# Float64 weights to fp32 by bytes on ScalarE, first slices ahead of the rows, even folds queued later, in a spectral two-MLP kernel

## The chip, the cores and the metric

One core of one Trainium2 chip. The metric is the device time of one launch in microseconds (us), the median of several runs; beside it stands one profiled execution, whose trace is read here.

## What is computed

```python
X = np.fft.fft(np.fft.fft(x, axis=1), axis=2).real      # x: 2 x 3008 x 256, fp32
x = X.reshape(6016, 256)
h = x @ w_in;  x = (np.maximum(h, 0) ** 2) @ w_out      # layer 1: 256 -> 2048 -> 256
h = x @ w_in2; y = (h - np.tanh(h)) @ w_out2            # layer 2: the same sizes
```

The weights arrive as float64. They have to become fp32 on the chip before anything else can use them.

## The kernel before

**Stages.** The 3008-point transform is done with matmuls against cosine and sine tables, on rows of `x` that have been added and subtracted ("folded") so that few distinct rows remain. The 256-point transform along the other axis is multiplied into layer 1's weights. Layer 1 runs over 8 blocks of about 376 columns (4 for each batch) and over 16 slices of 128 hidden units; layer 2 runs over the same blocks and slices, with its weights prepared during the last part of layer 1. Nearly every fp32 product is made of three matmuls on rounded halves, a high part and the remainder.

**The start.** `load_x` brings the rows of one third (two DMAs of 512 KB, added together on VectorE and GpSimd), `load_table` a table (752 KB), `fold` folds. The first five steps of a fold give the odd rows `xo`; the later steps (L319 to L328) give the even rows `xf`. `dft_pair` multiplies the odd rows with the tables, `pair_evac` takes the result out of PSUM into `uv`.

**One slice of weights.** `load_raw` loads a slice (512 KB, two 32-bit words for each number) into one of four `stage` buffers. `conv_abs` (ScalarE, L219) makes `val`, the high word's magnitude scaled so that its exponent fits; `val` has three buffers. `conv` (VectorE) shifts the low word right by 29 (L227), joins these bits with the shifted `val` (L229) and puts the sign in (L231). After L231 the stage buffer is free, and the next DMA for it may start. Then TensorE transforms the slice (`transform_in`, L247), ScalarE takes the high parts (L235, L250) and VectorE the remainders (L238, L255); `middle_load` moves one column by DMA, and `middle_add` and `clear_middle` on GpSimd finish it.

**One step of layer 1.** `front` multiplies slice and columns (TensorE, L352 to `w`); `mid` combines them on VectorE (L490 `pb`, L491 and L492 `h`), then ScalarE makes relu, the squared high part `gh` and the square (L498, L499, L500); `late` makes the remainder `gl` (L509; VectorE for block 0's first eight slices, GpSimd for all later ones); `back` multiplies by the second weights (L520). The first three slices skip the combination (`vneg`, L496). The slices 2 to 15 are converted and split while the steps of block 0 and 1 already run (`MADE` says at which step). The table `STEPS` sets the order: block 0's slices 0 to 3, block 1's 16 slices, block 0's slices 4 to 15, then block 2 to 7.

**Background work.** `bg0` finishes the even rows (L319 to L328, then `split_even`), `bg1` loads and folds the second batch (accumulating DMAs on GpSimd's queue, L288), `bg3` (`make_w2`) converts layer 2's 16 slices. A scheduler orders the instructions of each engine by readiness; `tc.issue_after(ins)` puts the instructions of its block that run on the engine of `ins` behind `ins` in that engine's order. Here `ins` is the latest L492, on VectorE, so ScalarE, GpSimd and SP are not held by it.

Of the kernel before, what the change touches and what calls it, by code (L numbers as in the profile page):

```python
# [138 lines left out]
def spectral_mlps(  # L139
# [62 lines left out]
    def wt_alloc(layer, f):  # L202
        wt[f] = main.tile([128, 4, 256], F32R, tag=f"wt{f}", name=f"wt{layer}_{f}")
# [2 lines left out]
        wt_alloc(2, f)  # L206
        sp.dma_start(f32(wt[f]).rearrange("p a n -> p (a n)"), saved[f])

    def load_raw(layer, f, eng=sp):
        t = stage()  # L210
        eng.dma_start(t.bitcast(I32), (w1 if layer == 1 else w2)[f].bitcast(I32))
        raw[layer, f] = t.bitcast(I32).rearrange("p (n t) -> p n t", t=2)

    def conv_abs(layer, f):
        v = main.tile([128, 512], F32, tag="val", name="val", bufs=3)
        val[layer, f] = v
        return act.activation(v, raw[layer, f][:, :, 1].bitcast(F32), AF.Abs, scale=2.0**-112)  # L219

    def conv(layer, f):

        r = raw.pop((layer, f))
        lo, hi = r[:, :, 0], r[:, :, 1]
        y = main.tile([128, 512], I32, tag="p", name="cy")
        u = val[layer, f].bitcast(I32)
        dve.tensor_scalar(y, lo, 29, None, ALU.logical_shift_right)  # L227
        yield
        dve.scalar_tensor_tensor(u, u, 3, y, ALU.logical_shift_left, ALU.bitwise_or)  # L229
        yield  # L230
        dve.scalar_tensor_tensor(u, hi, -(2**31), u, ALU.bitwise_and, ALU.bitwise_or)  # L231
        yield

    def split_hi(f, i, src):
# [5 lines left out]
    def transform_in(f, p):  # L240


        v = val[1, f]
        for m in range(2):
            for kt in range(2):
                cs = slice(kt * 128, (kt + 1) * 128)
                pe.matmul(p[:, m, 384:], wtab[:, kt, m, :], v[:, cs], start=(kt == 0), stop=(kt == 1))  # L247
# [94 lines left out]
    def load_table(blk, t):  # L342
        c = BLOCKS[blk][1]
        u = ring(f"tab{t}")
        sp.dma_start(f32(u)[:, :, :NC[c]], tabs_d[c][t])
        tab.setdefault(blk, []).append(u)
# [216 lines left out]
    def make_w2():  # L563

        for f in range(2):
            load_raw(2, f)
        yield
        for f in range(NF):
            conv_abs(2, f)
            yield  # L570
            yield from conv(2, f)
            if f + 2 < NF:
                load_raw(2, f + 2)
            v = val[2, f].rearrange("p (i n) -> p i n", i=2)
            u = main.tile([128, 2, 2, 256], F32R, tag="stage", name="w2", bufs=4)
            act.copy(u[:, :, 0], v)
            yield
            dve.tensor_tensor(u[:, :, 1], v, f32(u[:, :, 0]), ALU.subtract)
            sp.dma_start(saved[f], f32(u).rearrange("p i h n -> p (i h n)"))
            yield  # L580
            if f % 2 == 0:
# [12 lines left out]
            yield  # L594
            dve.tensor_tensor(u[:, 1], y, f32(u[:, 0]), ALU.subtract)
            sp.dma_start(sums_d[f // 2], f32(u).rearrange("p h n -> p (h n)"))
            yield
# [148 lines left out]
    yt = {}  # L746


    def weights1(f, p):

        wt_alloc(1, f)
        transform_in(f, p)
        split_hi(f, 2, val[1, f][:, 256:])
        split_transformed_hi(f, p)
        split_lo(f, 2, val[1, f][:, 256:])
        split_transformed_lo(f, p)

    pool.memset(sign, -1.0)
    pool.memset(sign[0:1], 1.0)
# [4 lines left out]
    for f in range(2):  # L764
        wps[0, f] = psw()

    for t in range(3):
        load_x(0, t)
        if t == 2:
            load_raw(1, 0)  # L770
            conv_abs(1, 0)
        load_table(0, t)
    sp.dma_start(wtab, wtab_d[:, :, :, :])
    for f in range(1, 5):
        load_raw(1, f)
    folds = [fold(0, t) for t in range(3)]
    step(folds[0], 5)
    step(folds[1], 5)
    step(conv(1, 0))
    step(folds[2], 5)  # L780
    for t in range(3):
        dft_pair(0, t)
    load_raw(1, 5)
    conv_abs(1, 1)
    weights1(0, wps[0, 0])
    middle_load(0)
    step(conv(1, 1))
    conv_abs(1, 2)
    pe0 = pair_evac(0)
    step(pe0, 1)  # L790
    n = NC[BLOCKS[0][1]]
    vneg = ring("vneg")
    for i in range(2):
        act.activation(vneg[:, i, :n], f32(uv[0][0][:, 1, i, :n]), AF.Copy, scale=sign)
    weights1(1, wps[0, 1])
    middle_load(1)
    step(conv(1, 2))
    conv_abs(1, 3)
    step(pe0)
    middle_add(0)  # L800

# [26 lines left out]
    for i in range(-2, NS - 2):  # L828
        blk, f = STEPS[i] if i >= 0 else (0, i)
        if i == max(MADE) + 2:  # L830
            wstack.close()
            pools["w"] = wstack.enter_context(tc.tile_pool(name="psb", bufs=2, space=PSUM))
        look(i + 2)
        if i in MADE:
            p = wps[STEPS[i + 2]]
            w = MADE[i]
            wt_alloc(1, w)
            transform_in(w, p)
            split_transformed_hi(w, p)

        if (blk, f) in DFT:
            for b2 in DFT[blk, f]:
                if b2 == 4:
                    step(bg1)
                    for t in range(3):
                        dft_pair(4, t)
                    step(pair_evac(4))
                else:
                    step(bg0 if b2 < 4 else bg2)
                    dft_mm(b2)  # L850
                    dft_evac(b2)
            look(i + 3)
        mids = mid(*STEPS[i + 2])
        step(mids, 1)
        if i >= 0:
            back(blk, f)
        if i >= 0 and ends(blk, f):
            evac(blk, blk == 0 and f == NF - 1)
        step(mids)
        if i >= -1:  # L860
            late(*STEPS[i + 1])

        if i + 4 in MADE and i + 4 > 1:
            load_raw(1, MADE[i + 4])
        if i in MADE:
            split_transformed_lo(w, p)
            split_hi(w, 2, val[1, w][:, 256:])
        if i + 2 in MADE and i + 2 > -1:
            conv_abs(1, MADE[i + 2])
        if i in MADE:  # L870
            split_lo(w, 2, val[1, w][:, 256:])
            middle_load(w)
        if i == -2:
            middle_add(1)
        if i - 1 in MADE:
            middle_add(MADE[i - 1])
        if i + 1 in MADE and i + 1 > -2:
            step(conv(1, MADE[i + 1]))

        if i >= 8:  # L880
            with tc.issue_after(last_mid[0].ins):
                if i < NF + HALF:
                    step(bg0, 1)
                elif i < 3 * NF:
                    step(bg1, 2)
                else:
                    if blk == 3:
                        step(bg2, 1)
                    step(bg3, 2)
        if blk == NBLK - 1:  # L890
            if f > 0:
                restore(f - 1)
            if f >= 8:
# [65 lines left out]
```

## Time and profile before

| | |
|---|---|
| median of 3 runs | 1008.41 us (1007.89 to 1009.72) |
| profiled execution, its own time | 1006.97 us |
| its span in the trace | 1005.1 us |
| TensorE busy | 963.3 us, 96% |
| VectorE busy | 787.4 us, 78% |
| ScalarE busy | 726.7 us, 72% |
| GpSimd busy | 251.6 us, 25% |
| chain that ended last | 80% TensorE, 12% VectorE, 3% issue, 2% ScalarE, 2% DMA |

TensorE is busy nearly all the time, so the time is its work plus what it waits, plus what it loses at a lower granted clock. A share over the whole span hides where that is: the stages have different limits, and are read one by one. The profile names TensorE PE (its weight loads PEld), VectorE DVE, ScalarE ACT, GpSimd POOL, and SP the queue that issues most DMAs.

### The profile page before, as it was taken

How to read it: one execution, taken by the hardware profiler on the slowest of the kernel's cores; microseconds unless marked ns; L12 is line 12 of the kernel's file. 1: busy time of each engine (PE TensorE's matmuls, PEld its weight loads, DVE VectorE, ACT ScalarE, POOL GpSimd, SP SyncE). 2: the span in 40 equal slices, each digit the busy share in tenths (PEclk: the TensorE clock that was granted, in tenths of full speed). 3: DMA queues.
4: the chain of work that ended last, by engine and by line, in shares of the span. 5: the costliest groups of instructions: out<-in, count | busy, mean ns of one | idle time of the engine just before them, and what ended most of it. 6: DMA issues, size and time to landing. Idle time of an engine off the chain costs nothing.

```text
span 1005.1 us, 15446 instructions
## 1 busy us (share of the span) xinstructions
PE 963.3 (96%) x5542; PEld 950.5 (95%) x5542; DVE 787.4 (78%) x1483; ACT 726.7 (72%) x1289; POOL 251.6 (25%) x171
## 2 busy tenths in 40 slices
PE   4998899899999999999999999999999999999998
PEld 3888898899999999999999999999999999999998
DVE  6999679757988688997576978769787797877766
ACT  2886767787888778897866767667676676766665
POOL 1144614653566546565500000000000000000000
PEclk9999999999999999999999999999999999999999
DMA  8674240205332422417620100001000010000000
GB/s 308 212 228 126 53 142 25 32 1 217 130 130 106 145 85 109 175 73 274 207 94 1 62 1 30 34 1 62 1 32 31 1 63 1 3 29 1 32 1 31
DMA packets 36332, 82.66 MB, mean 82 GB/s; under 512 B 7328, under 2 KB 21152, under 8 KB 36256
## 3 DMA queue, kind: packets, MB, share of 16 engines
q1 hardware_dynamic: 35280, 79.34, 22.5%
q0 software_dynamic: 976, 2.34, 1.4%
q8 instruction: 43, 0.70, 0.3%
q14 instruction: 33, 0.27, 0.1%
HBM read 55.97 MB, written 25.69 MB: 81 GB/s over the span
## 4 chain that ended last, share of the span: by engine, by line
PE 80%; DVE 12%; issue 3%; ACT 2%; DMA 2%; POOL 0%; SPq 0%; DVEq 0%; POOLq 0%; ACTq 0%
PE w L352 32%; PE a L352 29%; PE a L520 18%; DVE pb L490 2%; DVE h L491 2%; DVE h L492 1%; DMA p<-x 1%; DVE val L231 1%; DVE val L229 1%; DMA stage<-w 1%; ACT gh L499 1%; DVE p L321 1%; DVE wt L238 1%; PE w L247 1%; DMA mcol<-wt 0%
## 5 line engine op out<-in xcount | busy, mean ns | idle before, releaser
L509 POOL TENSOR_TENSOR gl<-h,gh 128x752 fp32r<-128x752 f32 (+1 forms) x120 | 230.0, 1925 | 195.2 <-ACT h L500 135.3
L352 PE MATMUL a<-gh,wt 128*128 128x376 f32 (+1 forms) x1024 | 259.7, 335 | 0.0
L520 PE MATMUL a<-gh,wt 128*128 128x376 f32 (+1 forms) x1024 | 204.4, 341 | 15.1 <-ACT gh L499 5.8
L520 PEld LDWEIGHTS a<-gh,wt 128*128 128x128 f32 x1024 | 179.4, 191 | 21.0 <-ACT gh L499 8.7
L352 PEld LDWEIGHTS a<-gh,wt 128*128 128x128 f32 x1024 | 184.7, 188 | 0.0
L352 PE MATMUL a<-gl,wt 128*128 128x376 f32 (+1 forms) x512 | 171.7, 335 | 0.0
L352 PE MATMUL w<-x,sums 128*128 128x376 f32 (+1 forms) x768 | 163.5, 334 | 0.0
L352 PE MATMUL w<-uv,wt 128*128 128x376 f32 (+1 forms) x777 | 157.1, 337 | 1.7 <-POOL wt L259 1.0
L498 ACT ACTIVATE h<-h 128x752 f32<-128x752 f32 (+1 forms) x125 | 103.8, 831 | 59.8 <-DVE h L492 59.1
L673 DVE TENSOR_TENSOR gl<-h,gh 128x376 fp32r<-128x376 f32 (+1 forms) x256 | 138.2, 545 | 11.2 <-ACT gh L671 10.6
L671 ACT CAST gh<-h 128x376 fp32r<-128x376 f32 (+1 forms) x256 | 129.3, 507 | 18.5 <-DVE h L669 17.6
L667 ACT ACTIVATE tanh<-h 128x376 f32<-128x376 f32 (+1 forms) x192 | 99.3, 519 | 56.6 <-DVE h L663 51.9
L352 PEld LDWEIGHTS w<-uv,wt 128*128 128x128 f32 x777 | 136.8, 190 | 2.8 <-POOL wt L259 1.3
L669 DVE TENSOR_TENSOR h<-h,tanh 128x376 f32<-128x376 f32 (+1 forms) x192 | 106.4, 555 | 40.0 <-ACT tanh L667 34.7
L352 PEld LDWEIGHTS w<-x,sums 128*128 128x128 f32 x768 | 135.5, 188 | 0.2 <-ACT u L701 0.2
L490 DVE SCALAR_TENSOR_TENSOR pb<-ub,w,w 128x376 f32<-128x376 f32 (+1 forms) x125 | 75.1, 601 | 56.5 <-PE w L352 48.6
L520 PE MATMUL a<-gl,wt 128*128 128x376 f32 (+1 forms) x512 | 109.1, 336 | 0.5 <-POOL gl L509 0.5
L500 ACT ACTIVATE h<-h 128x752 f32<-128x752 f32 (+1 forms) x128 | 106.8, 834 | 3.0
L499 ACT ACTIVATE gh<-h 128x752 fp32r<-128x752 f32 (+1 forms) x128 | 106.9, 835 | 2.9
L663 DVE TENSOR_TENSOR h<-u,w 128x376 f32<-128x376 f32 (+1 forms) x128 | 69.4, 542 | 38.8 <-ACT u L701 38.8
L352 PEld LDWEIGHTS a<-gl,wt 128*128 128x128 f32 x512 | 96.4, 188 | 0.4 <-DVE gl L673 0.3
L520 PEld LDWEIGHTS a<-gl,wt 128*128 128x128 f32 x512 | 90.8, 190 | 0.8 <-POOL gl L509 0.8
(98 smaller groups left out, 1082.6 us busy)
## 6 DMA issues: line engine op xcount, KB each, us to landing
stage<-w SPq DMA_DIRECT2D x32, 512.0 KB, 3.7
tab<-tab SPq DMA_DIRECT2D x12, 752.0 KB, 7.2
w2s<-w SPq DMA_DIRECT2D x16, 512.0 KB, 2.6
wt<-w2s SPq DMA_DIRECT2D x16, 512.0 KB, 3.6
sums<-sums SPq DMA_DIRECT2D x15, 512.0 KB, 3.8
tab<-tab SPq DMA_DIRECT2D x6, 756.0 KB, 5.4
x<-y SPq DMA_DIRECT2D x12, 376.0 KB, 3.6
x2f<-x SPq DMA_DIRECT2D x6, 752.0 KB, 4.7
```

Of the source, the lines that this page charges most:

```text
L352: pe.matmul(dst, a, r, start=(first and i == 0), stop=(last and i == 3 * len(terms) - 1), **kw)
L490: dve.scalar_tensor_tensor(pb[:, :n], ub[:, :n], w128[:, f:f + 1], bank(p, 0)[:, :n], ALU.mult, ALU.add)
L498: act.activation(h[:, :, :n], h[:, :, :n], AF.Relu)
L499: act.activation(gh[:, :, :n], h[:, :, :n], AF.Square)
L500: act.activation(h[:, :, :n], h[:, :, :n], AF.Square)
L509: eng.tensor_tensor(gl[:, :, :n], h[:, :, :n], f32(gh[:, :, :n]), ALU.subtract)
L520: pe.matmul(acc[1, blk][m][s][:, :n], wt[f][:, wi, m * 128:(m + 1) * 128], g[:, s, :n], start=first and k == 0, stop=last and k == len(par ...
L663: dve.tensor_tensor(h, c, d, ALU.add)
L667: act.activation(th, c, AF.Tanh)
L669: dve.tensor_tensor(h, c, th, ALU.subtract)
L671: act.copy(gh, h)
L673: dve.tensor_tensor(gl, h, f32(gh), ALU.subtract)
```

## The change

The shift of the low word on VectorE is gone. In its place ScalarE reads the low word's top byte and writes it, scaled by 1/32 and rounded down, over the low word in the stage buffer. VectorE keeps two instructions: the sign is joined to these bits in place, then the shifted `val`. ScalarE's first function is Copy instead of Abs, since the sign is masked later.

At the start, slice 0 is loaded and converted ahead of the rows, slice 1's raw words go to a buffer of the `uv` pair, the small table `wtab` moves ahead of two big tables, and the transforms of slices 0 and 1 stand ahead of the last part of the odd rows' transform. `vneg` takes the `uv` buffer of the raw slice.

The last even fold, which before was traced without `issue_after` and could be placed early, is now held behind the step's L492; and after step 14 three background steps are made for each step instead of one.

```diff
-    def conv_abs(layer, f):
+    def conv_parts(layer, f):
+        r = raw[layer, f]
         v = main.tile([128, 512], F32, tag="val", name="val", bufs=3)
         val[layer, f] = v
-        return act.activation(v, raw[layer, f][:, :, 1].bitcast(F32), AF.Abs, scale=2.0**-112)
+        act.activation(v, r[:, :, 1].bitcast(F32), AF.Copy, scale=2.0**-112)
+        first = r.rearrange("p n t -> p (n t)").bitcast(U8).rearrange("p (n t) -> p n t", t=8)[:, :, 3]
+        act.activation(r[:, :, 0], first, AF.Copy, scale=2.0**-5, bias=-15.5 / 32)
     def conv(layer, f):
-        r = raw.pop((layer, f))
-        lo, hi = r[:, :, 0], r[:, :, 1]
-        y = main.tile([128, 512], I32, tag="p", name="cy")
+        y = raw.pop((layer, f))[:, :, 0]
         u = val[layer, f].bitcast(I32)
-        dve.tensor_scalar(y, lo, 29, None, ALU.logical_shift_right)
+        dve.scalar_tensor_tensor(y, u, -(2**31), y, ALU.bitwise_and, ALU.bitwise_or)
         yield
         dve.scalar_tensor_tensor(u, u, 3, y, ALU.logical_shift_left, ALU.bitwise_or)
-        yield
-        dve.scalar_tensor_tensor(u, hi, -(2**31), u, ALU.bitwise_and, ALU.bitwise_or)
         yield
...
-    for t in range(3):
-        load_x(0, t)
-        if t == 2:
-            load_raw(1, 0)
-            conv_abs(1, 0)
-        load_table(0, t)
+    load_raw(1, 0)
+    conv_parts(1, 0)
+    step(conv(1, 0))
+    load_x(0, 0)
+    load_table(0, 0)
+    load_x(0, 1)
     sp.dma_start(wtab, wtab_d[:, :, :, :])
-    for f in range(1, 5):
+    load_raw(1, 1)
+    load_x(0, 2)
+    load_table(0, 1)
+    load_table(0, 2)
+    for f in range(2, 5):
         load_raw(1, f)
...
-                    step(bg0 if b2 < 4 else bg2)
+                    with tc.issue_after(last_mid[0].ins):
+                        step(bg0 if b2 < 4 else bg2)
...
-                    step(bg0, 1)
+                    step(bg0, 1 if i <= max(MADE) else 3)
```

The scheduler decides where the instructions come to stand. Three places of the program are shown; in the changed kernel the numbers of the same statements are four higher (L490 is L494); L225 and L227 are its two conversion instructions on ScalarE, L233 and L235 the two on VectorE.

**VectorE, about the combination of the steps at which the even fold of the first third is done** (L319 and L321 there). Before, the three instructions between L321 and the next L490 convert slice 13:

```order
L490 SCALAR_TENSOR_TENSOR pb<-ub,w_69,w 128x376
L238 TENSOR_TENSOR wt_12_883<-val,wt_12_883 128x256
L491 TENSOR_TENSOR h<-w,pb 128x376
L492 TENSOR_TENSOR h<-pb,w 128x376
L321 TENSOR_TENSOR p<-p 128x256
L227 TENSOR_SCALAR cy<-stage 128x512
L229 SCALAR_TENSOR_TENSOR val<-val,cy 128x512
L231 SCALAR_TENSOR_TENSOR val<-stage,val 128x512
L490 SCALAR_TENSOR_TENSOR pb<-ub,w_69,w 128x376
```

Now, from the same L490 (L494) on:

```order
L494 SCALAR_TENSOR_TENSOR pb<-ub,w_69,w 128x376
L242 TENSOR_TENSOR wt_13_922<-val,wt_13_922 128x256
L495 TENSOR_TENSOR h<-w,pb 128x376
L496 TENSOR_TENSOR h<-pb,w 128x376
L325 TENSOR_TENSOR p<-p 128x256
L233 SCALAR_TENSOR_TENSOR stage<-val,stage 128x512
L235 SCALAR_TENSOR_TENSOR val<-val,stage 128x512
L494 SCALAR_TENSOR_TENSOR pb<-ub,w_69,w 128x376
```

The two instructions after L325 (before: L321) now convert slice 14. The conversion of slice 13 stands a step earlier, and its remainder (`wt_13`) where `wt_12` stood. Counted from the seventh to the last instruction ahead of the 13th L490 (six steps), VectorE had 4 of L227, 4 of L229, 5 of L231 and 4 of L238; now it has 3 of L233, 3 of L235 and 5 of L242 (the former L238); the rest is the same.

**ScalarE, about its first conversion for layer 2** (the only L219 here). Before, it stands between the relu of one step and its `gh`:

```order
L498 ACTIVATE h<-h 128x2x376
L499 ACTIVATE gh<-h 128x2x376
L500 ACTIVATE h<-h 128x2x376
L498 ACTIVATE h<-h 128x2x376
L219 ACTIVATE val<-stage 128x512
L499 ACTIVATE gh<-h 128x2x376
L250 CAST wt_15_1071<-w 128x256
```

Now it stands, with its second half, behind the whole of an earlier step and a cast of the even rows:

```order
L502 ACTIVATE h<-h 128x2x376
L503 ACTIVATE gh<-h 128x2x376
L254 CAST wt_14_971<-w 128x256
L504 ACTIVATE h<-h 128x2x376
L339 CAST xe_1011<-xf_824 128x512
L225 ACTIVATE val<-stage 128x512
L227 ACTIVATE stage<-stage 128x512
L502 ACTIVATE h<-h 128x2x376
L503 ACTIVATE gh<-h 128x2x376
```

Counted by relus (L498, L502) from the first one, it stood after the 13th and now stands after the 11th.

**ScalarE, where the odd rows' transform leaves PSUM** (`dt` is the copy out of PSUM, `uv` the operand of the first products of layer 1). Before, both copies are together and one conversion stands ahead of the first `uv`:

```order
L219 ACTIVATE val<-stage 128x512
L427 COPY dt<-a_180 128x376
L427 COPY dt<-a_178 128x376
L219 ACTIVATE val<-stage 128x512
L438 CAST uv<-dt 128x376
L235 CAST wt_1_272<-val 128x256
L438 CAST uv<-dt 128x376
```

Now a whole conversion (slice 3) stands between the two copies, and more work between the two casts to `uv`:

```order
L225 ACTIVATE val<-stage 128x512
L227 ACTIVATE stage<-stage 128x512
L431 COPY dt<-a_175 128x376
L225 ACTIVATE val<-stage 128x512
L227 ACTIVATE stage<-stage 128x512
L431 COPY dt<-a_173 128x376
L442 CAST uv<-dt 128x376
L239 CAST wt_2_309<-val 128x256
L804 ACTIVATE vneg<-uv,sign 128x376
L442 CAST uv<-dt 128x376
```

The conversions of slices 2 and 3, two instructions each, are now all ahead of the first cast to `uv`. In the whole order of ScalarE, the second halves (L227) of the slices 4 to 15 follow, all of them ahead of the seventh relu L502; in the order of SP, layer 2's first raw slice still stands behind the three first DMAs of the second batch's rows, and the table that was issued just ahead of it now comes after it.

## Rows read from the trace of the kernel before

**Rows 1.** One row of the page's part 1: busy time, share, instructions

```profile
...
PE 963.3 (96%) x5542; PEld 950.5 (95%) x5542; DVE 787.4 (78%) x1483; ACT 726.7 (72%) x1289; POOL 251.6 (25%) x171
...
```

**Rows 2.** Windows: PE, PEld, DVE, ACT, POOL busy (x), PEclk, DMA share, GB/s

```profile
0.00:29.00 29.00, 13.49 (x67) 11.30 (x67) 19.22 (x42) 8.36 (x17) 4.94 (x11) 1.00 0.80 292
29.00:56.00 27.00, 25.71 (x161) 24.42 (x160) 25.22 (x52) 22.84 (x47) 7.67 (x16) 1.00 0.70 225
56.00:73.40 17.40, 15.30 (x96) 14.33 (x95) 17.30 (x33) 14.05 (x24) 7.80 (x9) 1.00 0.67 217
73.40:101.00 27.60, 23.56 (x139) 23.26 (x138) 27.05 (x47) 18.46 (x29) 14.50 (x18) 0.94 0.53 140
101.00:126.60 25.60, 22.29 (x120) 21.39 (x120) 15.98 (x30) 18.21 (x26) 15.88 (x14) 0.93 0.18 44
126.60:240.00 113.40, 108.80 (x626) 105.69 (x625) 80.39 (x149) 83.93 (x114) 52.44 (x29) 1.00 0.24 75
240.00:470.00 230.00, 222.53 (x1267) 219.57 (x1268) 198.84 (x339) 192.29 (x262) 128.44 (x66) 0.99 0.37 132
470.00:1005.00 535.00, 531.58 (x3079) 530.57 (x3077) 403.38 (x799) 368.58 (x777) 19.97 (x11) 1.00 0.11 38
```

**Rows 3.** Groups of instructions by line, 20 to 101 us

```profile
...
L231 DVE SCALAR_TENSOR_TENSOR val<-stage,val 128x512 int32<-128x512 int32 x16 | 13.2, 827 | 0.1
...
L238 DVE TENSOR_TENSOR wt<-val,wt 128x256 fp32r<-128x256 f32 x16 | 9.2, 573 | 0.5 <-ACT wt L235 0.3
...
L219 ACT ACTIVATE val<-stage 128x512 f32<-128x512 f32 x15 | 10.1, 671 | 0.8 <-DVE wt L238 0.8
...
L321 DVE TENSOR_TENSOR p<-p 128x256 f32<-128x256 f32 x2 | 3.0, 1509 | 0.0
...
L319 DVE TENSOR_TENSOR p<-p 128x256 f32<-128x256 f32 x2 | 2.7, 1336 | 0.0
...
L227 DVE TENSOR_SCALAR cy<-stage 128x512 int32<-128x512 int32 x16 | 6.7, 416 | 0.0
...
```

**Rows 4.** Timeline, 76 to 92 us, three engines

```profile
...
82.31 2.60 DVE L321 TENSOR_TENSOR p<-p 128x256 f32<-128x256 f32 x1
...
86.01 2.14 DVE L231 SCALAR_TENSOR_TENSOR val<-stage,val 128x512 int32<-128x512 int32 x1
...
82.47 2.15 POOL L509 TENSOR_TENSOR gl<-h,gh 128x752 fp32r<-128x752 f32 x1
...
85.30 2.30 POOL L509 TENSOR_TENSOR gl<-h,gh 128x752 fp32r<-128x752 f32 x1 [0.34 <-POOL w L273]
...
88.20 2.08 PE L247 MATMUL w<-val,wtab 128*128 128x128 f32 x8 [4.04 <-DVE val L231]
...
```

**Rows 5.** Timeline, 97 to 112 us, and one row of the DMA issues

```profile
...
97.61 0.33 SPq L211 DMA_DIRECT2D stage<-w  x1
...
105.19 0.66 ACT L219 ACTIVATE val<-stage 128x512 f32<-128x512 f32 x1 [3.32 <-DMA stage<-w]
...
106.63 1.65 PE L520 MATMUL a<-gh,wt 128*128 128x376 f32 x8 [1.49 <-ACT gh L499]
...
110.47 0.78 PE L520 MATMUL a<-gh,wt 128*128 128x376 f32 x3 [1.52 <-ACT gh L499]
...
stage<-w SPq DMA_DIRECT2D x5, 512.0 KB, 4.4
...
```

**Rows 6.** Timeline, 25 to 29 us, ScalarE and TensorE

```profile
...
26.41 0.47 ACT L427 COPY dt<-a 128x376 f32<-128x376 f32 x1 [0.37 <-PE a L352]
...
27.35 0.50 ACT L438 CAST uv<-dt 128x376 fp32r<-128x376 f32 x1
...
28.61 0.61 PE L352 MATMUL w<-uv,wt 128*128 128x376 f32 x2
...
```

**Rows 7.** Waits of PE, 240 to 470 us; a timeline row at 441.84

```profile
...
PE a L520 <- DVE y L551: 3.7, 2, 2.0
...
441.84 1.98 DVE L227 TENSOR_SCALAR cy<-stage 128x512 int32<-128x512 int32 x1
...
```

More of the change, by code (lines that the diff above doesn't have):

```diff
@@ L12 @@
 I32 = mybir.dt.int32
+U8 = mybir.dt.uint8
 AF = mybir.ActivationFunctionType
@@ L207, in restore, with load_raw @@
         sp.dma_start(f32(wt[f]).rearrange("p a n -> p (a n)"), saved[f])
-    def load_raw(layer, f, eng=sp):
-        t = stage()
-        eng.dma_start(t.bitcast(I32), (w1 if layer == 1 else w2)[f].bitcast(I32))
+    def load_raw(layer, f):
+        if (layer, f) == (1, 1):
+            t = f32(main.tile([128, 2, 2, NM], F32R, tag="uv", name="raw", bufs=2)).rearrange("p a b n -> p (a b n)")[:, :1024]
+        else:
+            t = stage()
+        sp.dma_start(t.bitcast(I32), (w1 if layer == 1 else w2)[f].bitcast(I32))
         raw[layer, f] = t.bitcast(I32).rearrange("p (n t) -> p n t", t=2)
-    def conv_abs(layer, f):
+    def conv_parts(layer, f):
+        r = raw[layer, f]
         v = main.tile([128, 512], F32, tag="val", name="val", bufs=3)
         val[layer, f] = v
-        return act.activation(v, raw[layer, f][:, :, 1].bitcast(F32), AF.Abs, scale=2.0**-112)
+        act.activation(v, r[:, :, 1].bitcast(F32), AF.Copy, scale=2.0**-112)
+        first = r.rearrange("p n t -> p (n t)").bitcast(U8).rearrange("p (n t) -> p n t", t=8)[:, :, 3]
+        act.activation(r[:, :, 0], first, AF.Copy, scale=2.0**-5, bias=-15.5 / 32)
     def conv(layer, f):
-        r = raw.pop((layer, f))
-        lo, hi = r[:, :, 0], r[:, :, 1]
-        y = main.tile([128, 512], I32, tag="p", name="cy")
+        y = raw.pop((layer, f))[:, :, 0]
         u = val[layer, f].bitcast(I32)
-        dve.tensor_scalar(y, lo, 29, None, ALU.logical_shift_right)
+        dve.scalar_tensor_tensor(y, u, -(2**31), y, ALU.bitwise_and, ALU.bitwise_or)
         yield
         dve.scalar_tensor_tensor(u, u, 3, y, ALU.logical_shift_left, ALU.bitwise_or)
-        yield
-        dve.scalar_tensor_tensor(u, hi, -(2**31), u, ALU.bitwise_and, ALU.bitwise_or)
         yield
@@ L568, in make_w2 @@
         for f in range(NF):
-            conv_abs(2, f)
+            conv_parts(2, f)
             yield
@@ L746, in spectral_mlps, with split_weights @@
     yt = {}
-    def weights1(f, p):
-        wt_alloc(1, f)
-        transform_in(f, p)
+    def split_weights(f, p):
         split_hi(f, 2, val[1, f][:, 256:])
@@ L756, in weights1 @@
         split_transformed_lo(f, p)
+        middle_load(f)
     pool.memset(sign, -1.0)
@@ L777, in spectral_mlps @@
     step(folds[0], 5)
+    wt_alloc(1, 0)
+    transform_in(0, wps[0, 0])
     step(folds[1], 5)
-    step(conv(1, 0))
+    dft_pair(0, 0)
+    conv_parts(1, 1)
+    step(conv(1, 1))
+    dft_pair(0, 1)
+    wt_alloc(1, 1)
+    transform_in(1, wps[0, 1])
     step(folds[2], 5)
-    for t in range(3):
-        dft_pair(0, t)
+    dft_pair(0, 2)
     load_raw(1, 5)
[L784 to L788, printed above, removed]
+    split_weights(0, wps[0, 0])
+    conv_parts(1, 2)
     pe0 = pair_evac(0)
@@ L791, in spectral_mlps @@
     n = NC[BLOCKS[0][1]]
-    vneg = ring("vneg")
+    vneg = main.tile([128, 2, 2, NM], F32R, tag="uv", name="vneg", bufs=2)[:, 0]
     for i in range(2):
         act.activation(vneg[:, i, :n], f32(uv[0][0][:, 1, i, :n]), AF.Copy, scale=sign)
-    weights1(1, wps[0, 1])
-    middle_load(1)
+    split_weights(1, wps[0, 1])
     step(conv(1, 2))
-    conv_abs(1, 3)
+    conv_parts(1, 3)
     step(pe0)
@@ L868, in spectral_mlps @@
         if i + 2 in MADE and i + 2 > -1:
-            conv_abs(1, MADE[i + 2])
+            conv_parts(1, MADE[i + 2])
         if i in MADE:
```

## The prediction

> **What bounds the kernel now.** I read the shares first, then the same busy times stretch by stretch, since one share hides different limits. TensorE is busy 963.3 us of a span of 1005.1 [rows 1]. The stages show where the other 42 us are [rows 2]: the reader is to take the length of a stretch less TensorE's busy time as its idle time, and one less the granted clock, times the length, as what the lower clock cost. From 470 us on TensorE stands still for 3.4 of 535 us; there is nothing to win in layer 2. The first 29 us hold 15.5 us of start. Between them:
>
> - 29 to 73.4 us: 1.3 + 2.1 = 3.4 us idle. VectorE is busy 42.5 of 44.4 us, ScalarE 36.9.
> - 73.4 to 101 us: 4.0 us idle and 0.06 x 27.6 = 1.7 us of clock. VectorE is busy 27.05 of 27.6 us.
> - 101 to 126.6 us: 3.3 us idle and 0.07 x 25.6 = 1.8 us of clock.
> - 126.6 to 470 us: 4.6 + 7.5 = 12.1 us idle, little clock.
>
> Which wait ends last in each? In the second one it is the conversion of a slice on VectorE: TensorE waits 4.04 us for L231, and after this pause its next eight matmuls of a transform take 2.08 us [rows 4]. That slice was late because VectorE instructions just ahead took 2.6 and 2.1 us: each began while GpSimd made a `gl`, or just before, and ended 0.3 to 0.6 us after it [rows 4]. I call this a hold. L319 and L321 have means of 1.3 and 1.5 us, where L238 on as many elements has 0.57 and the shift L227 on twice as many 0.42 [rows 3]. In the third one it is a DMA that ScalarE waits for: layer 2's first raw slice is issued at 97.61, and ScalarE stands 3.32 us until 105.19 with `gh` behind it, for which TensorE then waits 1.49 and 1.52 us [rows 5].
>
> **The change, part by part.** *Layer 1's conversion.* Each slice loses a shift of 0.42 us on VectorE and gets an activation on ScalarE, whose cost no row shows, since nothing here reads single bytes. The nearest is the conversion's other activation, L219, 0.67 us for the same 512 elements with a stride [rows 3]. Bounds: the 0.42 us of the shift below, twice L219, 1.3 us, above. I take 0.67, as the work is most like L219's. VectorE's in-place instruction writes with a stride what L231 read with one: 0.83 with holds as now, no change.
>
> *Start to 73.4 us.* Thirteen of the new activations (slices 3 to 15) stand between the first copy to `dt` and ScalarE's seventh relu, which closes this stretch: 13 x 0.67 = 8.7 us. ScalarE has 44.4 - 36.9 = 7.5 us free there [rows 2], and two first activations have moved ahead, 1.3 us. So ScalarE comes out full, 44.3 of 44.4 us, and takes VectorE's place as the limit. The start itself gets later: the slice ahead of the rows is 0.52 MB, 1.8 us at the stretch's 292 GB/s [rows 2], and the conversion of slice 3 between the two copies delays the second by two activations, 1.3 us, so that the cast to `uv`, now at 27.35, and TensorE's first products, now at 28.61, come some 1.2 us later [rows 6]. What pays for this: slices 0 and 1 are wholly made by then, and VectorE has lost 5 us of shifts. I take a gain of 0.5 us: at best all 3.4 us of idle time, at worst 1.8 + 1.2 = 3 us lost.
>
> *73.4 to 101 us.* By the order, VectorE has in the six steps from the seventh L490 on four shifts less (1.7 us), three conversion instructions less, since they have moved ahead (3 x 0.83 = 2.5 us), and one remainder L238 more (0.57 us [rows 3]): 27.05 - 3.6 = 23.4 us. TensorE by itself needs 27.6 - 5.7 = 21.9 us. So VectorE still sets the pace, for a gain of 27.6 - 23.4 = 4.2 us; and as the slice that TensorE waited for now stands a whole step earlier, one long hold no longer reaches TensorE, which can give all 5.7. I take 4.5, between 1 (the holds grow into the room) and 5.7.
>
> *101 to 126.6 us.* The load behind the 3.32 us is issued two steps earlier and ScalarE comes to it two relus earlier. In the trace 4.3 us lie between (97.61 to 101.87); now, by the order, a step's combination and ScalarE's relu, `gh`, two casts and a square, some 5 us. The load took 7.6 us here, the median of such loads is 4.4 [rows 5]; the table that was issued just ahead of it now follows it, so I expect it nearer the median, at 5.5. What is left is a wait of 0.5 and the second activation, about 1 of the 5.1 us of loss: a gain of 4.1, taken as 4. Bounds: 0 (7.6 us again, and one step less of room) and 5.1.
>
> *Even folds held back.* Seven instructions of the last fold leave the crowded time about 30 us for the steps at 111 to 123 us, where VectorE is busy only 16.0 of 25.6 us [rows 2]; the casts and GpSimd's remainders follow. Hidden by that room they cost nothing; without it, one hold of 2.6 us as in [rows 4] would show. Queue places: behind the later tables on SP stand only block outputs, and `vneg` in the `uv` pair frees a buffer for the tables.
>
> *126.6 to 470 us.* Sixteen slices of layer 2: VectorE 16 x 0.42 = 6.7 us less on 198.8 us, ScalarE 16 x 0.67 = 10.7 us more on 192.3 of 230 us [rows 2]. Both stay under the length, TensorE needs its time anyway. Only where TensorE waits for VectorE's copies at the ends of blocks (3.7 us in two waits [rows 7]) does this count: I take 1.5 us, between -2 (the new activation ahead of a `gh` or a copy) and 4.
>
> **A rule weighed.** One shift in the trace takes 1.98 us [rows 7]; the other 16 of the first slices average 0.416 [rows 3], so shifts are hardly ever held, the instructions that stay are. The Trainium skill, SBUF — State Buffer, "Who interferes with whom", says that a VectorE instruction with two SBUF inputs contends with a GpSimd instruction that reads SBUF, while one with a single input does so only in a two-port mode. That speaks against this change: by it the instruction removed is the cheaper one, and the two that remain are those that are held. The sum already goes by the rows' 0.42; had the shift carried the holds of L231, four of them would give 1.6 us more. The row at 1.98 says that a shift can be held too.
>
> **Sum.** 0.5 + 4.5 + 4 + 1.5 = 10.5 us off the profiled execution's 1006.97 (span 1005.1 and 1.9 around it): 996.5. The median of the runs shown is 1.4 us above that execution: 998.
>
> **Rivals.**
> *ScalarE is the new limit.* For: it comes out full in 29 to 73.4 us, with waits of its own that the sum leaves out. Against: its new work has room before 29 and after 73.4 us. If 3.5 us are lost there, 1001.5.
> *The wait for layer 2's slice stays.* For: ScalarE comes to it two relus earlier. Against: so does the load, with less ahead of it. Without those 4 us: 1002.
> *The holds take the room on VectorE.* GpSimd's work is unchanged, and each two-input instruction may meet it. Then 73.4 to 101 us gives 1 instead of 4.5 us: 1001.5.
> *Slower: the byte read is slow.* All 13 activations stand where ScalarE is full, so each microsecond more on one costs 13. No row shows one; L219 at 0.67 us with a stride of two words speaks against [rows 3]. At the upper bound of 1.3 us the time is 998 + 8 = 1006. The change is even where one takes 0.67 + 10.5/13 = 1.5 us, and slower by more than 0.2% from 1.63; at 2.0 it gives 998 + 17 = 1015.
> *It does nothing that can be measured:* the time is TensorE's, and waits removed come back elsewhere: 1008.
>
> **How the numbers follow.** 0.2% is 2.0 us, about what a measurement of this kernel can tell from no change. Chances: forecast 0.52 (994.5 to 1001), ScalarE 0.13, slice's wait 0.12, holds 0.10, slow byte read 0.05, nothing 0.05, better than 994.5 0.03. Two of the middle rivals together would come near 1005. The range 991 to 1006 takes in an activation of 1.3 us and leaves out a slower one, the change without effect and the best and worst sums, some 0.15. Faster 0.86, same 0.07, slower 0.07.
>
> **What would show it.** Right: the new activation near 0.67 us; no wait of TensorE for a conversion in the stretch that was 73.4 to 101 us, and its clock at 1.00 there; ScalarE near full from 29 us to its seventh relu; that relu at about the same time as now, 73.4 us; the first of layer 2's conversions with under 1 us of wait; the same TensorE work, and layer 2 unchanged to a microsecond. Wrong: an activation above 1 us, TensorE waiting for ScalarE's `gh` ahead of 73 us, or new waits at the ends of blocks from 240 us on.

## The result and the profile after

The changed kernel is slower: 1014.05 us (median of 5 runs, 1009.76 to 1016.54) against 1008.41 us (median of 5, 1006.50 to 1009.72). The ratio is 1.0057, with a 95% interval of 1.0032 to 1.0082. I had forecast 998 us, with 991 to 1006 as the range. The profiled execution of the changed kernel took 1013.33 us, its span is 1011.6 us.

First the row of busy times, and the windows of the changed kernel: up to 124 us at the events that bound [rows 2] (TensorE's first products, the seventh and the 13th relu, the 20th combination), then at 240 and 480 us. The lines named here have numbers 4 higher than before: L225 and L227 are the two activations of a conversion, L233 and L235 its VectorE instructions, L242 and L259 the remainders of weights, L494 to L496 the combination, L502 to L504 relu, `gh` and square, L513 `gl`, L524 the second layer's products, L555 the copies at the end of a block, L580 and L582 `w2`, L590 to L599 the sums, L627 and L629 the splits and L638 and L640 the differences of `make_x7`.

```profile
PE 969.4 (96%) x5542; PEld 956.5 (95%) x5542; DVE 788.2 (78%) x1451; ACT 742.6 (73%) x1321; POOL 244.3 (24%) x171
```

```profile
0.00:30.30 30.30, 14.07 (x66) 12.03 (x66) 19.46 (x40) 11.85 (x24) 4.05 (x13) 0.94 0.81 297
30.30:75.95 45.65, 44.47 (x273) 43.45 (x274) 40.60 (x69) 41.22 (x79) 14.98 (x23) 0.96 0.61 201
75.95:101.64 25.69, 21.68 (x124) 20.80 (x123) 22.80 (x40) 19.03 (x31) 14.88 (x17) 0.93 0.75 169
101.64:124.04 22.40, 20.59 (x119) 19.70 (x118) 18.68 (x36) 17.86 (x25) 15.10 (x13) 1.00 0.12 36
124.04:240.00 115.96, 111.95 (x633) 108.57 (x632) 84.18 (x153) 85.68 (x119) 52.62 (x29) 0.99 0.25 77
240.00:480.00 240.00, 228.64 (x1276) 225.05 (x1276) 200.51 (x323) 201.01 (x276) 124.52 (x67) 0.97 0.39 135
480.00:1011.60 531.60, 527.99 (x3060) 526.91 (x3058) 402.01 (x796) 365.92 (x774) 18.17 (x10) 1.00 0.10 34
```

To see where the time goes I compare the start of the n-th combination (L490, now L494) in both traces. The changed kernel is 2.1 us behind at the 7th, 0.15 behind at the 13th, 3.0 ahead at the 21st, 2.0 ahead at the 49th (237.89 against 239.85 us), and 6.7 us behind at the 121st (491.13 against 484.42); behind it the distance stays, 6.5 us at the end. The 49th and the 121st, first in the kernel before, then in the changed one:

```profile
239.85 0.60 DVE L490 SCALAR_TENSOR_TENSOR pb<-ub,w,w 128x376 f32<-128x376 f32 x1
484.42 0.61 DVE L490 SCALAR_TENSOR_TENSOR pb<-ub,w,w 128x376 f32<-128x376 f32 x1 [1.37 <-PE w L352]
```

```profile
237.89 0.60 DVE L494 SCALAR_TENSOR_TENSOR pb<-ub,w,w 128x376 f32<-128x376 f32 x1
491.13 0.61 DVE L494 SCALAR_TENSOR_TENSOR pb<-ub,w,w 128x376 f32<-128x376 f32 x1 [1.37 <-PE w L356]
```

So 8.7 us are lost between these two, from about 240 to 485 us, where layer 2's slices are converted beside the last blocks of layer 1, and where I had forecast a gain. The windows say in which form. The same window of the kernel before:

```profile
240.00:480.00 240.00, 232.53 (x1325) 229.57 (x1326) 204.33 (x349) 200.03 (x271) 134.24 (x70) 0.99 0.39 140
```

The changed kernel has 240.00 - 228.64 = 11.4 us of idle time there, the kernel before 7.5; by the granted clock the changed kernel loses 0.03 x 240 = 7.2 us, the kernel before 0.01 x 240 = 2.4. That is 3.9 + 4.8 = 8.7 us, though a clock rounded to 0.01 makes the second part uncertain by some 2 us. The waits of TensorE from 240 to 480 us:

```profile
PE a L524 <- ACT y L555: 5.2, 3, 3.5
PE a L524 <- ACT gh L503: 3.1, 3, 1.9
PE a L524 <- DVE y L555: 2.1, 1, 2.1
PE a L524 <- POOL gl L513: 1.0, 2, 0.5
```

The clock's part goes with the idle part: about the longest of these waits, which ends at 461.49, the granted clock of the window is down, as it is in the stretch of the waits at 403 and 406 us:

```profile
400.00:420.00 20.00, 16.69 (x85) 15.97 (x85) 19.87 (x31) 16.11 (x24) 7.52 (x6) 0.91 0.43 149
460.00:480.00 20.00, 18.51 (x92) 18.52 (x93) 11.05 (x22) 15.68 (x21) 9.07 (x5) 0.83 0.53 162
```

Who is late for the wait of 3.45 us? The timeline from 453.9 to 462.5 us, three engines ahead of TensorE:

```profile
454.07 1.82 POOL L513 TENSOR_TENSOR gl<-h,gh 128x756 fp32r<-128x756 f32 x1 [3.30 <-ACT h L504]
454.15 2.54 DVE L629 TENSOR_TENSOR x<-x2f,x 128x752 fp32r<-128x752 f32 x1
457.03 1.79 POOL L513 TENSOR_TENSOR gl<-h,gh 128x752 fp32r<-128x752 f32 x1 [1.14 <-PE a L524]
457.13 2.10 DVE L640 TENSOR_TENSOR x2f<-x2f 128x376 f32<-128x376 f32 x1
459.27 0.82 ACT L627 CAST x<-x2f 128x752 fp32r<-128x752 f32 x1 [2.36 <-DVE x2f L640]
460.98 0.83 ACT L555 COPY y<-a 128x378 f32<-128x378 f32 x2
461.49 1.31 PE L524 MATMUL a<-gh,wt 128*128 128x376 f32 x3 [3.45 <-ACT y L555]
```

Read it upwards. TensorE waits for ScalarE's copies; these stand in ScalarE's queue behind a relu and a cast, and the cast waits 2.36 us for a VectorE difference (L640, 0.54 us elsewhere); that one took 2.10 us, since it began 0.1 us after a `gl` of GpSimd and ended 0.4 us after it, and the VectorE instruction two places ahead of it had been held in the same way (0.93 us elsewhere). Other waits are alike: at 262 us `gh` stands behind a cast that waits for a held sum, at 379 us behind one that waits for a held L235, and at 406 us VectorE's own copies stand behind a held L582.

### The profile page after: what moved, and what is told of

It is laid out like the page before. It is cut to its first block, busy times and chain, and to the rows that moved or that the text cites. A ratio compares the mean times of both kernels' runs of the same rounds, so it can differ in the third digit from the quotient of the medians.

```text
span 1011.6 us, 15453 instructions
## 1 busy us (share of the span) xinstructions
PE 969.4 (96%) x5542; PEld 956.5 (95%) x5542; DVE 788.2 (78%) x1451; ACT 742.6 (73%) x1321; POOL 244.3 (24%) x171
## 4 chain that ended last, share of the span: by engine, by line
PE 79%; DVE 10%; ACT 6%; issue 4%; DMA 1%; POOL 1%; DVEq 0%; ACTq 0%; POOLq 0%
PE w L356 31%; PE a L356 30%; PE a L524 17%; DVE h L496 2%; DVE h L495 2%; DVE pb L494 1%; ACT gh L503 1%; DMA stage<-w 1%; ACT h L502 1%; ACT h L504 1%; DVE val L235 1%; DVE p L323 1%; ACT val L225 1%; POOL gl L513 1%; PE w L251 1%
## 5 line engine op out<-in xcount | busy, mean ns | idle before, releaser
L513 POOL TENSOR_TENSOR gl<-h,gh 128x752 fp32r<-128x752 f32 (+1 forms) x120 | 224.2, 1869 | 201.9 <-ACT h L504 159.1
L524 PE MATMUL a<-gh,wt 128*128 128x376 f32 (+1 forms) x1024 | 207.2, 344 | 16.2 <-ACT y L555 7.9
L524 PEld LDWEIGHTS a<-gh,wt 128*128 128x128 f32 x1024 | 181.8, 193 | 21.9 <-ACT y L555 9.1
L356 PE MATMUL w<-uv,wt 128*128 128x376 f32 (+1 forms) x777 | 160.4, 343 | 4.2 <-DVE wt L259 2.9
L356 PEld LDWEIGHTS w<-uv,wt 128*128 128x128 f32 x777 | 140.3, 195 | 5.6 <-issue 2.8
L502 ACT ACTIVATE h<-h 128x752 f32<-128x752 f32 (+1 forms) x125 | 103.7, 830 | 54.3 <-DVE h L496 53.7
L494 DVE SCALAR_TENSOR_TENSOR pb<-ub,w,w 128x376 f32<-128x376 f32 (+1 forms) x125 | 75.2, 601 | 54.8 <-PE w L356 49.5
L524 PE MATMUL a<-gl,wt 128*128 128x376 f32 (+1 forms) x512 | 109.7, 337 | 2.1 <-POOL gl L513 2.1
L504 ACT ACTIVATE h<-h 128x752 f32<-128x752 f32 (+1 forms) x128 | 106.8, 834 | 2.6
L524 PEld LDWEIGHTS a<-gl,wt 128*128 128x128 f32 x512 | 90.6, 190 | 3.7 <-POOL gl L513 3.7
```

Of the source, the lines that this page charges most:

```text
L356: pe.matmul(dst, a, r, start=(first and i == 0), stop=(last and i == 3 * len(terms) - 1), **kw)
L494: dve.scalar_tensor_tensor(pb[:, :n], ub[:, :n], w128[:, f:f + 1], bank(p, 0)[:, :n], ALU.mult, ALU.add)
L502: act.activation(h[:, :, :n], h[:, :, :n], AF.Relu)
L504: act.activation(h[:, :, :n], h[:, :, :n], AF.Square)
L513: eng.tensor_tensor(gl[:, :, :n], h[:, :, :n], f32(gh[:, :, :n]), ALU.subtract)
L524: pe.matmul(acc[1, blk][m][s][:, :n], wt[f][:, wi, m * 128:(m + 1) * 128], g[:, s, :n], start=first and k == 0, stop=last and k == len(par ...
```

## The experiments

I call a VectorE instruction held where it takes over 0.4 us more than the shortest of its line and shape in the stretch, and count from 240 to 470 us. In the kernel before these are 21 instructions, and all VectorE instructions together take 30.5 us beyond the shortest of their kind, which I call the sum of the holds; in the changed kernel 24 and 35.7 us. Each of them overlaps a `gl` of GpSimd. Of the 193 combinations L494 to L496 of the changed kernel, whose inputs come in part from PSUM, none is held (1.6 us in all). This count misses a line that is held every time; against the shortest of the same operation and shape on any line there are 23 held instructions with a sum of 33.6 us before, and 26 with 39.1 us in the changed kernel.

**e1_l2_old: layer 2's conversion as before, in the changed kernel.**

```
-            conv_parts(2, f)
+            conv_abs(2, f)
             yield
-            yield from conv(2, f)
+            yield from conv_old(2, f)      # shift, or, sign: three pauses
```

> The changed kernel with layer 2's slices converted as before (shift on VectorE, one activation, three pauses). Theory: all of the loss arises from 240 us on, in layer 2's conversion, so this kernel keeps the lead of 2 to 3 us at 240 us and has no loss behind it: 1004 to 1007 us. Rival: the loss there comes from the first 240 us, whose other order leaves the engines in another phase; then it stays near 1012 to 1015 us.

1005.2 us, ratio 0.9970 (0.9952 to 0.9988). The loss is gone, and the intervals are apart: it is made in layer 2's conversion.

**e2_l2_new: only layer 2's conversion new, in the kernel before.** The reverse edit.

> The kernel before with layer 2's conversion alone made new. Theory: this part alone loses 6 to 9 us, 1014 to 1018 us. Rival (the phase left by the first 240 us decides): within 2 us of the kernel before, 1006 to 1010 us. By the prediction's own term, 1.5 us gained: 1007 us.

1014.44 us, 1.0068 (1.0046 to 1.0091). That part alone, put into the older kernel, loses 6.9 us. The phase in which the first 240 us leave the engines isn't needed for it; TensorE's waits come at the same places (3.46 us for a copy at 462.81).

**e3_l2_pace: a third pause in layer 2's conversion.**

```
             yield from conv(2, f)
+            yield
```

> The changed kernel with a third pause in layer 2's conversion, so that a pair of slices takes 8.5 steps again and its VectorE instructions stand at other places against the block ends. Theory (places decide): the time moves by several us, to 1004 to 1009 us. Rival (the additional ScalarE activations ahead of the casts and copies cost the time wherever they stand): 1012 to 1015 us, unchanged.

1013.55 us, 1.0047 (1.0032 to 1.0063): no different from the changed kernel. My guess that the pace of 7.5 instead of 8.5 steps for a pair of slices puts instructions at the wrong places fell. Again 22 instructions are held, with a sum of 32.8 us (29 with 42.2 us by operation and shape); now L233 takes 7 of the 22.

**e4_l1_new: only layer 1's conversion new, in the kernel before.**

> The kernel before with layer 1's conversion alone made new; the start, the loads, the even folds and layer 2 as before. By the prediction, the 13 shifts less are worth their 0.42 us where VectorE sets the pace: some 2 to 4 us less in 73 to 101 us, 1004 to 1006 us. Rival (a hold by GpSimd isn't removed with the instruction, it meets the next one): within 1.5 us of the kernel before, 1007 to 1010 us.

1006.58 us, 0.9992 (0.9978 to 1.0007): between the two ranges, and nothing that can be measured. The shifts that are gone from layer 1 give at most 2.2 us.

**e5_act_only and e6_no_byte: the two engines apart.** The first adds only ScalarE's activation to e1_l2_old, the second takes it alone out of the changed kernel, where VectorE then takes the three bits from the raw word. VectorE's instructions are those of e1_l2_old and of the changed kernel, in nearly the same order.

```
+        scr = main.tile([128, 512], mybir.dt.bfloat16, tag="scr", name="scr", bufs=1)
+        act.activation(scr, first, AF.Copy, scale=2.0**-5, bias=-15.5 / 32)
...
+        if layer == 1:
             act.activation(r[:, :, 0], first, AF.Copy, scale=2.0**-5, bias=-15.5 / 32)
...
+            dve.scalar_tensor_tensor(y, y, 7, u, ALU.bitwise_and, ALU.bitwise_or)
```

> The kernel of e1_l2_old (layer 2 converted as before) with the additional byte activation of each slice of layer 2 put in as well, into a tile that nobody reads; the orders of the other engines stay as in e1_l2_old. Theory A (the additional 16 activations, 11 us on ScalarE, stand ahead of gh, casts and copies): all of the loss comes back, 1011 to 1015 us. Theory B (the shift that left VectorE took holds for which nobody waited; now other instructions take them): no loss, 1004 to 1007 us.

> The changed kernel without the byte activation in layer 2, so that the low bits of its weights are left out and its values are others; VectorE has the same instructions in the same order as in the changed kernel, ScalarE 16 activations less. Theory A (ScalarE): 1004 to 1007 us. Theory B (VectorE's order and the holds): 1011 to 1015 us, and VectorE's instructions from 240 to 470 us are again held for 33 to 37 us.

e5_act_only: 1007.36 us, 0.9992 (0.9977 to 1.0008). e6_no_byte: 1010.75 us, 1.0018 (1.0003 to 1.0032). Against e1_l2_old, ScalarE's part is 0.0022 x 1008.4 = 2.2 us, with intervals that overlap; VectorE's is 4.8 us, and the intervals are apart. Both together are 8.8, and the 1.8 us left over are within the uncertainty of about 3 us. Counted from the changed kernel backwards, ScalarE's part is 1.0057 - 1.0018, 3.9 us, and VectorE's is 1.0057 - 0.9992, 6.6 us. VectorE's is the larger either way. The traces say the same of the stretch itself: from the 49th to the 121st combination e1_l2_old takes 246.9 us, e5_act_only 246.0, e6_no_byte 251.2 and the changed kernel 253.2. With one trace of each, ScalarE's activations alone cost nothing there, and some 2 us on top of VectorE's new instructions. TensorE's waits from 240 to 480 us side with VectorE, first e5_act_only, then e6_no_byte:

```profile
PE a L545 <- DVE y L576: 3.7, 2, 2.0
PE a L545 <- ACT gh L524: 3.4, 4, 1.7
PE a L545 <- ACT y L576: 0.3, 1, 0.3
```

```profile
PE a L528 <- ACT y L559: 5.8, 3, 3.4
PE a L528 <- ACT gh L507: 2.9, 3, 1.5
PE a L528 <- DVE y L559: 2.1, 1, 2.1
PE a L528 <- POOL gl L517: 0.5, 1, 0.5
```

7.4 us of waits with ScalarE's 16 activations, as without them (8.0 in e1_l2_old); 11.3 us with VectorE's new instructions, among them those of 2.1 and 3.4 us of the changed kernel, though ScalarE has less to do there than before. Theory A falls as the main cause. Theory B's size was a little high: its range for e6_no_byte is missed by 0.3 us, that for e5_act_only by 0.4, and the sum of the holds of e6_no_byte is 40.1 us, above its range too.

**e7_after_memset and e8_l2old_memset: GpSimd reads nothing.** From block 3 on:

```
+        if blk >= 3:
+            pool.memset(f32(gl[:, :, :n]), 0.0)
+        else:
             eng.tensor_tensor(gl[:, :, :n], h[:, :, :n], f32(gh[:, :, :n]), ALU.subtract)
```

> The changed kernel with GpSimd's remainder gl from block 3 on replaced by a memset, which reads nothing (the remainder is left out there). Theory B: without a GpSimd instruction that reads beside VectorE the holds of 36 us from 240 to 470 us fall below 5 us, the loss there is gone: 1002 to 1006 us. Theory A: holds don't matter, 1011 to 1015 us.

> The kernel of e1_l2_old with the same memset in place of the remainder from block 3 on. Theory B: without holds the kernel with the older conversion has the longer VectorE work, so it comes out within 1 us of e7_after_memset or behind it, 1001 to 1005 us. Theory A: some 7 to 9 us ahead of e7_after_memset, as e1_l2_old is ahead of the changed kernel.

994.86 us, 0.9864 (0.9841 to 0.9888), and 992.91 us, 0.9849 (0.9832 to 0.9866): no difference between the two conversions that can be measured, where e1_l2_old and the changed kernel are 8.8 us apart. Not one VectorE instruction is held (1.8 and 2.1 us in all), TensorE doesn't stand still for a moment, and from the 49th to the 121st combination the two take 233.5 and 233.4 us. The window of e7_after_memset, and its GpSimd group from 240 to 470 us:

```profile
240.00:480.00 240.00, 240.00 (x1390) 239.38 (x1389) 177.78 (x344) 215.52 (x297) 53.29 (x74) 1.00 0.44 151
```

```profile
L514 POOL MEMSET gl<- 128x752 f32 (+1 forms) x70 | 51.0, 730 | 186.7 <-PE a L527 186.7
```

Both times lie 7 us or more below the ranges that I gave: I had expected back only what the change had lost, and the kernel before has holds of its own. ScalarE is at its busiest here, 215.5 of 240 us, and it costs nothing. All idle time of this stretch, in either kernel, goes with GpSimd's remainders. A memset is also shorter than a remainder (0.73 against some 1.9 us) and waits for neither `h` nor `gh`, so the runs show that the remainders cause it, but not by themselves that reading does. TensorE's waits for `gl` itself were a small part of it: 1.0 of the 11.4 us in the changed kernel, none in the kernel before.

**e9_gl_at_ends and e10_sums_pool: fewer holds from 240 us on,** both on e1_l2_old.

```
-        eng = dve if blk == 0 and f < NF // 2 else pool
+        eng = dve if blk == 0 and f < NF // 2 or blk >= 3 and f in (0, 1, NF - 1) else pool
...
-            dve.tensor_tensor(s1, a21, a22, ALU.add)
+            pool.tensor_tensor(s1, a21, a22, ALU.add)      # and s2, s3, s4
```

> The kernel of e1_l2_old with the remainder gl of each block's last and first two steps made by VectorE instead of GpSimd from block 3 on (14 instructions of 0.93 us, as those of block 0). Theory (a GpSimd remainder that runs beside VectorE holds it, and it costs where a block's copies stand behind): the holds ahead of the copies are gone, 3 to 5 us off e1_l2_old, 1000 to 1003 us. Rival (VectorE has no room for 13 us more, or waits there for ScalarE's squares): 1005 to 1009 us.

> The kernel of e1_l2_old with layer 2's 32 sums of 128x128 made by GpSimd instead of VectorE. Theory (each VectorE instruction of that stretch with all its inputs in SBUF can be held, and an instruction on GpSimd cannot): some 6 of the 22 held instructions go, 1 to 4 us off e1_l2_old, 1001 to 1004 us. Rival (ScalarE's cast of the sums now waits behind GpSimd's remainders, and GpSimd is busy longer beside VectorE): 1005 to 1010 us.

1003.32 us, 0.9948 (0.9932 to 0.9965), and 1004.52 us, 0.9962 (0.9943 to 0.9981). e9 comes out 2.2 us ahead of e1_l2_old, less than expected and with intervals that overlap (the trace has 15 such remainders on VectorE from block 3 on, not 14): waits for copies fall from 5.7 to 2.5 us, those for `gh` rise from 2.3 to 4.5, and 24 instructions are still held, at other places. e10 has 19 held instead of 22, and no gain that can be told from e1_l2_old.

**e11_folds_as_before: the even folds not held back,** on e1_l2_old.

```
-                    with tc.issue_after(last_mid[0].ins):
-                        step(bg0 if b2 < 4 else bg2)
+                    step(bg0 if b2 < 4 else bg2)
...
-                    step(bg0, 1 if i <= max(MADE) else 3)
+                    step(bg0, 1)
```

> The kernel of e1_l2_old with the even folds as in the kernel before (not held back). By the prediction they cost or gain nothing: within 1.5 us of e1_l2_old, 1004 to 1007 us. Rival: without it VectorE is again crowded from 73 to 101 us, 1 to 3 us slower, 1006 to 1009 us.

1002.73 us, 0.9941 (0.9919 to 0.9963): not slower but 2.9 us faster than e1_l2_old, though the intervals overlap. Its trace is 6.7 us ahead of the kernel before at the 49th combination, e1_l2_old 3.6. One place, first in e1_l2_old, then in e11_folds_as_before (L530 is `gl`, L572 the copies):

```profile
54.19 1.82 POOL L530 TENSOR_TENSOR gl<-h,gh 128x752 fp32r<-128x752 f32 x1 [0.26 <-ACT h L521]
54.44 1.85 DVE L259 TENSOR_TENSOR wt<-val,wt 128x256 fp32r<-128x256 f32 x1
57.72 1.07 PE L541 MATMUL a<-gh,wt 128*128 128x376 f32 x4 [1.18 <-DVE y L572]
```

```profile
53.97 0.68 DVE L233 SCALAR_TENSOR_TENSOR stage<-val,stage 128x512 int32<-128x512 int32 x1
54.04 2.30 POOL L530 TENSOR_TENSOR gl<-h,gh 128x752 fp32r<-128x752 f32 x1 [0.47 <-ACT h L521]
54.57 0.53 DVE L512 TENSOR_TENSOR h<-w,pb 128x376 f32<-128x376 f32 x1
55.03 0.53 DVE L513 TENSOR_TENSOR h<-pb,w 128x376 f32<-128x376 f32 x1
55.48 0.99 DVE L572 COPY y<-a 128x376 f32<-128x376 f32 x2
```

The same `gl` meets a remainder (0.41 us when free) in the one, and the copies behind it are late. In the other L233 began 0.07 us ahead of `gl`; it takes its free 0.68 us, `gl` is the longer one (2.30 against 1.82 us), and the instructions that follow read PSUM and are not held. This is one place; what the rest of the 2.9 us is made of was not followed up.

**e12_combined:** e11_folds_as_before with the edit of e9_gl_at_ends.

> The kernel of e11_folds_as_before (layer 2 converted as before, even folds as before, layer 1's new conversion and the new start kept) with the remainders of each block's last and first two steps on VectorE from block 3 on, as in e9_gl_at_ends. Theory (the two gains lie in different stretches, up to 130 us and from 280 us on, and add): 1.5 to 3 us off e11_folds_as_before, 0.991 to 0.993 of the kernel before, 999 to 1001.5 us. Rival (which VectorE instructions are held falls anew with every change of phase, so gains don't add): 0.994 to 0.997, 1002 to 1006 us.

1000.34 us, 0.9931 (0.9909 to 0.9954). It beats both kernels, by 0.7 and 1.3%. It is 1.0 us ahead of e11_folds_as_before by the ratios, where 1.5 to 3 were expected, and can't be told apart from it, so whether the two gains add stays open.

## Why the prediction was wrong

The runs make a ladder from the kernel before to the changed one: layer 1's conversion alone 0.9992, with the new start 0.9941, with the even folds held back 0.9970, with layer 2's conversion 1.0057. In us of 1008.41 these steps are -0.8, -5.1, +2.9 and +8.8, the first uncertain by 1.5 us, the others by about 3. By the stretches of the forecast, 0.5 + 4.5 + 4 + 1.5 us, the two traces have -2.6 + 2.0 + 3.1 - 9.2 = -6.7 us.

- **126.6 to 470 us, +1.5 forecast: this step failed.** It gave -8.8 us by the ladder, -9.2 by the two traces (from the 20th combination to the 116th). I costed the edit as busy time (6.7 us less on VectorE, 10.7 more on ScalarE, both under the length), and took it that what leaves VectorE can only help. The removed shift did not carry 0.42 us here. The groups from 240 to 470 us, first the kernel before (L227 the shift), then the changed one:

```profile
L231 DVE SCALAR_TENSOR_TENSOR val<-stage,val 128x512 int32<-128x512 int32 x16 | 15.3, 954 | 0.0
L227 DVE TENSOR_SCALAR cy<-stage 128x512 int32<-128x512 int32 x16 | 15.0, 935 | 0.0
L229 DVE SCALAR_TENSOR_TENSOR val<-val,cy 128x512 int32<-128x512 int32 x16 | 14.3, 892 | 0.5
L578 DVE TENSOR_TENSOR w<-val,w 128x512 fp32r<-128x512 f32 x16 | 13.6, 851 | 0.0
```

```profile
L582 DVE TENSOR_TENSOR w<-val,w 128x512 fp32r<-128x512 f32 x16 | 17.2, 1077 | 3.0 <-ACT w L580 3.0
L235 DVE SCALAR_TENSOR_TENSOR val<-val,stage 128x512 int32<-128x512 int32 x16 | 15.8, 989 | 0.2
L233 DVE SCALAR_TENSOR_TENSOR stage<-val,stage 128x512 int32<-128x512 int32 x16 | 14.2, 889 | 0.0
```

  The shift took 15.0 us, 8.0 of them in 6 holds. A dearer shift alone would have made the forecast gain larger; what failed is that its holds would go with it. I had taken its mean, 416 ns, from a stretch [rows 3] in which GpSimd's `gl` runs 19.6 of 75 us (10 instructions, 26 to 101 us), against 128.4 of 230 us here (66 instructions), and set the one row of 1.98 us aside [rows 7]. With the shift gone the holds did not go (26 instead of 23, as counted above): they fell on L582, on the sums and on L629 and L640, behind which casts, `gh` and copies stand. The lower bound of -2 was for a new activation ahead of a `gh`; that a hold moves to a worse place had no bound at all, and the rival on holds spoke of 73 to 101 us only.
- **The rule weighed.** I read the exemption of instructions with a single input in the Trainium skill, SBUF — State Buffer, "Who interferes with whom", as one for the shift. The same section counts `tensor_scalar` among the instructions that can enter a two-port mode and so contend; the Trainium skill, VectorE: DVE Perf Modes, "Mode 2×_2P — use both read ports for one tensor", says that this mode spends both read ports on the one source. Here the trace and the rule agree: 6 of 16 shifts were held. [Rows 3] had a sign of it: 416 ns for 512 elements, where instructions with two inputs take 0.68 us at their shortest. I drew the wrong conclusion; the right one alone would not have given the loss, since it doesn't say what the next instruction meets.
- **Start to 73.4 us, +0.5:** the 7th combination came 2.1 us later and the seventh relu 2.6 us (75.95 against 73.35), within the bounds. TensorE's first products began at 30.30 instead of 28.61, 1.7 us later where I had 1.2, and the granted clock was 0.83 from 20 to 40 us, which I had not foreseen. ScalarE did not come out full, 41.2 of 45.7 us, where I had 44.3 of 44.4; TensorE itself was busy for 44.5.
- **73.4 to 101 us, +4.5:** the gain was 2.0 us. The wait of 4.04 us is gone, as forecast, but the granted clock is 0.93 there, where I had named 1.00, and "one long hold no longer reaches TensorE" failed: the next instruction in line was held, and TensorE waited 2.24 us behind it.

```profile
91.48 2.46 DVE L242 TENSOR_TENSOR wt<-val,wt 128x256 fp32r<-128x256 f32 x1 [0.19 <-ACT wt L239]
91.53 2.12 POOL L513 TENSOR_TENSOR gl<-h,gh 128x752 fp32r<-128x752 f32 x1
95.33 2.19 PE L356 MATMUL w<-uv,wt 128*128 128x376 f32 x6 [2.24 <-DVE wt L259]
```

- **101 to 126.6 us, +4:** the mechanism was right and the size near, 3.1 us. The first slice of layer 2 is loaded from 91.00 instead of 97.61 us, and ScalarE converts it at 98.04 without a wait. Of these gains 1.0 us is lost again up to 240 us.
- **Even folds held back, 0:** about -2.9 us, at the edge of what the runs can tell, and near the 2.6 us that I had put on one hold without the room; "Hidden by that room they cost nothing" looked at where the instructions go and not at what then stands beside `gl` in the steps that they leave.
- **The new activation** is as forecast (L227), so the rival of the slow byte read is dead:

```profile
L225 ACT ACTIVATE val<-stage 128x512 f32<-128x512 f32 x30 | 20.2, 673 | 4.4 <-DVE sums L591 4.1
L227 ACT ACTIVATE stage<-stage 128x512 int32<-128x512 uint8 x30 | 20.1, 676 | 1.9 <-DMA stage<-w 1.9
```

Layer 2 itself is unchanged, and "new waits at the ends of blocks from 240 us on", named as what would make the prediction wrong, is what came.

What stays open: why VectorE's new order puts its holds at worse places. It isn't the pace (e3_l2_pace). The sum of the holds goes with it, but doesn't give the size: by operation and shape the four kernels with layer 2's new conversion and GpSimd's remainders have 38.2 to 43.6 us of it, the others with these remainders 30.9 to 36.6; yet e6_no_byte has the 43.6 and loses less than the changed kernel with 39.1. Why there are more holds isn't shown either. A run that keeps VectorE's instructions and changes their places one by one wasn't made. Nor is it settled whether the 2.2 us of ScalarE's activations are more than the spread.

## What to carry to other kernels

Here an instruction on VectorE with all its inputs in SBUF cost its shortest time only where it didn't meet a `gl` of GpSimd: take its duration from the stretch in which it runs, and ask who stands behind it, and behind the next one in line, if that one is held in its place. Removing a held instruction removed its own time here, not the holds. Where holds make all the idle time, look at what GpSimd does beside VectorE before taking work off VectorE: here 12 us lie there (e8_l2old_memset against e1_l2_old), though that kernel leaves the remainders out, and moving some of them to VectorE gave 2.2 and 1.0 us, neither clear of the noise.

## What the runs showed of the hardware

A VectorE shift with one input in SBUF, 0.42 us when free, takes 1.87 to 1.98 us when it begins just behind a `gl` of GpSimd (0.13 to 0.23 us), five times in 16 in the kernel before from 240 to 470 us. In the same stretch 24 VectorE instructions with all inputs in SBUF began inside a `gl`, at least 0.5 us before its end: 22 were held and the other two took 0.39 us longer than the shortest, each until 0.15 to 0.55 us after the `gl`; of 94 that read PSUM none was. It goes the other way round too: the 19 `gl` that began while such an SBUF instruction had 0.2 us or more to run took 1.96 to 2.53 us, the other 47 took 1.79 to 1.98. In this stretch the one that began later waited; that isn't without exception, since at 82.31 us [rows 4] L321 began 0.16 us earlier than a `gl` and was held all the same. Beside 70 GpSimd memsets of 0.73 us no VectorE instruction was held. An activation that reads single bytes with a stride of eight takes 0.68 us for 512 elements, as long as one that reads words with a stride of two.
